# A gate brought ahead of the attention output, and GpSimd's pooling moved in among its load issues

## The chip, the cores and the metric

The kernel runs on one core of a Trainium2 chip. The metric is the device time of one execution in microseconds (us), lower is better.

The core has five engines with separate queues: PE (TensorE, matrix products; its products land in eight PSUM banks), ACT (ScalarE), DVE (VectorE), POOL (GpSimd) and SP. In the traces below ACT, DVE and POOL take their instructions in the order of the program (ACT in slot 1: Ln at 33.53, Relu at 34.20, Exp at 34.68 us, as written). Here POOL issues nearly all loads and also does some additions.

## The reference

For each of 8 batches and 8 heads (576 positions, head size 64), two attentions are added: one on q, k, v averaged over groups of four positions, and one in a band of seven positions. The result, as 4608 rows of 512, goes through a gated layer:

```python
out_d   = softmax_attn(mean4(q), mean4(k), mean4(v))       # 144 positions
x       = repeat4(out_d) + banded_attn(q, k, v)            # |i - j| < 4
gate    = np.maximum(x @ w_gate, 0.0)                      # 512 -> 1536
out     = (gate * (x @ w_val)) @ w_out                     # 1536 -> 512
```

## The kernel before

Heads are taken in pairs (`hp`, 0 to 31), rows in nine chunks of 512. After a short fill, the kernel runs in *slots*: slot `s` holds a quarter of a chunk's gated layer (three blocks of 128 columns), and the attention of pair `hp = s + 4` woven between. The gated layer of one block is two groups of four matmuls into a pair of banks, then a *gate*: Relu on ACT out of the first bank, and a multiply with the second bank on DVE.

```python
    def emit_h(c, jj, pp, parts=...):                 # pp: pair of banks
        h1, h2 = pair(pp)[:, 0, :], pair(pp)[:, 1, :]
        ...                                           # 4 + 4 matmuls
        def gate():
            r1 = ffn.tile([128, TCH], FP16, name="r1", tag="r1")
            nc.scalar.activation(out=r1, in_=h1, func=AF.Relu)
            nc.vector.tensor_tensor(out=gT[c % 2][:, jj, :], in0=r1, in1=h2, op=ALU.mult)
        return gate
```

The last gate of a slot is not emitted there. It is handed to the next slot as `gate`, the *pending gate*. In slots 1 to 5 the next slot passed it into the attention output `emit_s2t`, whose normalisation is a reciprocal by way of logarithms:

```python
    def emit_s2t(hp, between):
        ...                                           # sums to banks 4, 5; products to banks 2, 3
        r, x = rden[r2], xn[r2]
        nc.scalar.activation(out=r, in_=ps[:, 4:6, 0:360], func=AF.Ln)
        between()                                     # the pending gate: Relu on ACT, multiply on DVE
        nc.scalar.activation(out=r, in_=r, func=AF.Exp, scale=-1.0)
        nc.vector.tensor_tensor(out=x, in0=ps[:, 2:4, 0:360], in1=r, op=ALU.mult)   # xn
        emit_xsum(hp)                                                               # xT
```

The scores of the next pair (`emit_s1`, banks 4 to 7) are exponentiated on ACT and masked on DVE in two pieces; the mask multiply has two inputs in SBUF:

```python
            nc.vector.tensor_tensor(out=o, in0=o, in1=_sap(masks_sb, ...), op=ALU.mult)   # ee
```

POOL adds up v in groups of four (pairs 9 and up), in two additions which also have both inputs in SBUF: `v2` (about 1.17 us) and then `v1` (about 0.72 us). Before, both stood at the head of a slot, in front of that slot's load issues:

```python
    def emit_slot(s, gate):
        c, jj, hp = s // 4, 3 * (s % 4), s + LEAD
        if NVP <= hp + 1 < NP:
            emit_vd_pool(hp + 1)                      # v2, v1 on POOL
        emit_in(hp + 4)                               # POOL: issues q, k, then v
        ...
        if s <= 5:
            if s == 5:
                emit_pool(hp)
            elif s < 4:
                emit_vd(hp, 1)
            emit_s2t(hp - 1, gate)
        ...                                           # s 1 to 3: emit_h(jj, pair 0), emit_s1,
                                                      # emit_h(jj + 1, pair 1: banks 2, 3), ...
                                                      # s >= 5: emit_s1 earlier, then emit_s2w(hp)
```

The softmax here doesn't subtract the row's maximum and nothing guards it: scores larger than these inputs give would overflow.

## Time and profile before

| kernel before | |
|---|---|
| time | 354.89 us, median of 3 runs (354.39 to 355.57); 354.70 with a fourth run |
| span of the trace | 352.6 us |
| PE busy | 343.5 us |
| granted PE clock (1.00 is full speed) | 1.00 |

The busy times of the engines, from the first part of the page (engine, us, share of the span, instructions):

```profile
PE 343.5 (97%) x2947; PEld 187.0 (53%) x2947; DVE 248.3 (70%) x397; ACT 214.0 (61%) x370; POOL 189.5 (54%) x233
```

PE is the limit, so only the time in which PE waits can be won. This is its table of waits, cut to three lines (line of PE, whom it waited for, then total us, times, longest us):

```profile
...
PE ps L505 <- DVE xn L426: 0.8, 3, 0.3
...
PE ps L505 <- DVE gT L521: 0.5, 1, 0.5
PE ps L448 <- DVE ee L326: 0.3, 1, 0.3
```

The first is in slots 1 to 3, once each, the last is in slot 5; the middle one is in the tail, after slot 27. The rest of the table lies in the fill. The wait in slot 1, on PE's timeline (start us, duration us, engine, line, operation, tiles, shapes, count, and in brackets the idle time before and who ended it):

```profile
35.93 0.29 PE L314 MATMUL ps<-qkT 64*128 64x96 f16 x6
36.48 1.02 PE L505 MATMUL ps<-xT,wg_sb 128*128 128x512 f16 x4 [0.26 <-DVE xn L426]
```

The bracket says 0.26 us. From start to start it is 36.48 - 35.93 = 0.55 us, while in slots 0 and 4, without a wait, the same step takes 0.22 us; so the loss is 0.33 us (PE's ends are modelled, so starts are the better measure). What PE waits for is `xn`, which reads banks 2 and 3. Here is what ACT did meanwhile:

```profile
33.03 0.37 ACT L294 CAST vd<-ps 72x256 f16<-72x256 f32 x1 [1.52 <-PE ps L287]
33.53 0.77 ACT L423 ACTIVATE rden<-ps 128x720 f32<-128x720 f32 x1
34.20 0.59 ACT L520 ACTIVATE r<-ps 128x512 f16<-128x512 f32 x1
34.68 0.81 ACT L425 ACTIVATE rden<-rden 128x720 f32<-128x720 f32 x1
```

and DVE:

```profile
34.83 0.69 DVE L521 TENSOR_TENSOR gT<-r,ps 128x512 f16<-128x512 f16 x1 [3.24 <-ACT r L520]
35.52 0.91 DVE L426 TENSOR_TENSOR xn<-ps,rden 128x720 f16<-128x720 f32 x1
```

The Relu of the pending gate (L520) stands between Ln (L423) and Exp (L425), and its multiply (L521) stands ahead of xn (L426). Exp ends at 34.68 + 0.81 = 35.49 us and the multiply at 35.52 us: either could be what holds xn up. The trace does not say which, since a wait is put down to the one that came last.

Slot 5 has the other wait. DVE's two masks, POOL's additions, and PE's attention output (one timeline each):

```profile
71.39 2.31 DVE L326 TENSOR_TENSOR ee<-ee,cst_sb 112x576 f16<-112x576 f16 x2
```

```profile
71.03 1.46 POOL L274 TENSOR_TENSOR v<-v 72x512 f32<-72x512 f16 x1
72.56 0.82 POOL L275 TENSOR_TENSOR vd<-v 72x256 f16<-72x256 f32 x1
```

```profile
73.27 0.23 PE L456 MATMUL ps<-ed,vd 72*128 72x72 f16 x2
73.76 0.29 PE L448 MATMUL ps<-ee,vw 112*128 112x96 f16 x3 [0.26 <-DVE ee L326]
```

Two masks take 0.82 us elsewhere. Here they took 2.31 us, and PE had to wait for the second: 0.49 us between these two starts, against 0.07 us in slot 6, a loss of 0.42 us. From about 80 to 279 us PE has no wait at all.

### The profile page before, as it was taken

How to read it: one execution, taken by the hardware profiler on the slowest of the kernel's cores; microseconds unless marked ns; L12 is line 12 of the kernel's file. 1: busy time of each engine (PE TensorE's matmuls, PEld its weight loads, DVE VectorE, ACT ScalarE, POOL GpSimd, SP SyncE). 2: the span in 40 equal slices, each digit the busy share in tenths (PEclk: the TensorE clock that was granted, in tenths of full speed). 3: DMA queues.
4: the chain of work that ended last, by engine and by line, in shares of the span. 5: the costliest groups of instructions: out<-in, count | busy, mean ns of one | idle time of the engine just before them, and what ended most of it. 6: DMA issues, size and time to landing. Idle time of an engine off the chain costs nothing.

```text
span 352.6 us, 7540 instructions
## 1 busy us (share of the span) xinstructions
PE 343.5 (97%) x2947; PEld 187.0 (53%) x2947; DVE 248.3 (70%) x397; ACT 214.0 (61%) x370; POOL 189.5 (54%) x233
## 2 busy tenths in 40 slices
PE   6999999999999999999999999999999999999996
PEld 3665555545545555555555544455555465655575
DVE  5894666687786677788887787776777655354581
ACT  3867776676677766666666667667667533333332
POOL 8986557999999877777778877722100000000000
PEclk9999999999999999999999999999999999999999
DMA  9999999999999999999999999940000000101013
GB/s 153 168 171 187 182 194 153 180 167 194 176 146 166 171 131 131 134 134 118 134 119 138 113 131 140 123 95 30 32 31 32 33 30 30 46 30 46 15 47 119
DMA packets 168770, 40.26 MB, mean 114 GB/s; under 512 B 150080, under 2 KB 165664, under 8 KB 168736
## 3 DMA queue, kind: packets, MB, share of 16 engines
q0 software_dynamic: 132960, 22.93, 86.1%
q1 hardware_dynamic: 32176, 10.55, 17.6%
q10 hardware_dynamic: 3600, 6.32, 5.3%
q8 instruction: 23, 0.38, 0.5%
q14 instruction: 11, 0.09, 0.1%
HBM read 46.45 MB, written 9.44 MB: 159 GB/s over the span
## 4 chain that ended last, share of the span: by engine, by line
PE 89%; DVE 4%; ACT 4%; DMA 1%; issue 1%; POOLq 0%
PE ps L505 50%; PE ps L530 18%; PE ps L592 8%; PE ps L448 3%; PE ps L248 2%; PE ps L314 2%; PE ps L303 2%; PE ps L456 2%; DMA qk<-in_k_dram 1%; DVE xn L426 1%; ACT rden L423 1%; DVE xo L375 1%; ACT rden L425 1%; DVE ee L326 1%; ACT r L520 1%
## 5 line engine op out<-in xcount | busy, mean ns | idle before, releaser
L505 PE MATMUL ps<-xT,wg_sb 128*128 128x512 f16 x432 | 111.5, 379 | 0.9 <-DVE xn L426 0.8
L505 PE MATMUL ps<-xT,wv_sb 128*128 128x512 f16 x432 | 111.2, 379 | 0.5 <-DVE gT L521 0.5
L521 DVE TENSOR_TENSOR gT<-r,ps 128x512 f16<-128x512 f16 x108 | 71.8, 683 | 49.2 <-PE ps L505 32.4
L520 ACT ACTIVATE r<-ps 128x512 f16<-128x512 f32 x108 | 64.0, 593 | 38.2 <-PE ps L505 35.7
L530 PE MATMUL ps<-wo_sb,gT 128*128 128x512 f16 x288 | 70.1, 380 | 0.0
L505 PEld LDWEIGHTS <-wv_sb 128*128 128x128 f16 x432 | 42.1, 98 | 51.4 <-issue 0.8
L472 DVE TENSOR_TENSOR xn<-ps,rden 64x720 f16<-64x720 f32 x46 | 41.6, 905 | 39.2 <-ACT rden L469 38.5
L505 PEld LDWEIGHTS <-wg_sb 128*128 128x128 f16 x432 | 39.7, 97 | 39.5 <-issue 0.7
L323 ACT ACTIVATE ee<-ps 112x576 f16<-112x576 f32 x64 | 38.1, 647 | 26.2 <-PE ps L314 25.4
L466 ACT ACTIVATE rden<-ps 64x720 f32<-64x720 f32 x46 | 35.2, 764 | 12.9 <-PE ps L456 12.3
L530 PEld LDWEIGHTS <-gT 128*128 128x128 f16 x288 | 26.1, 98 | 30.0
L326 DVE TENSOR_TENSOR ee<-ee,cst_sb 112x576 f16<-112x576 f16 x64 | 40.8, 674 | 1.3 <-ACT ee L323 1.1
L275 POOL TENSOR_TENSOR vd<-v 72x256 f16<-72x256 f32 x23 | 17.7, 770 | 44.2 <-PE ps L456 43.5
L194 POOL DMA_DIRECT2D qk<-in_q_dram x46 | 34.1, 744 | 4.2 <-DMA wo_sb<-in_moe_w_out_dram 2.8
L194 POOL DMA_DIRECT2D qk<-in_k_dram x46 | 33.2, 728 | 0.6 <-DMA qk<-in_k_dram 0.4
L215 POOL DMA_DIRECT2D vw<-in_v_dram x30 | 28.4, 946 | 4.9 <-PE ps L396 1.4
L229 DVE TENSOR_REDUCE qkd<-qkT 128x288 f16<-128x1152 f16 x23 | 30.8, 1341 | 0.0
L274 POOL TENSOR_TENSOR v<-v 72x512 f32<-72x512 f16 x23 | 30.5, 1327 | 0.3
L538 ACT COPY y_sb<-ps 128x512 f32<-128x512 f32 x24 | 14.1, 587 | 17.2 <-PE ps L530 17.2
L431 DVE TENSOR_TENSOR xT<-xn 128x576 f16<-128x576 f16 x28 | 22.3, 798 | 0.2
L448 PE MATMUL ps<-ee,vw 112*128 112x96 f16 x276 | 20.4, 205 | 0.3 <-DVE ee L326 0.3
L332 ACT ACTIVATE ed<-ps 72x576 f16<-72x576 f32 x32 | 20.5, 642 | 0.0
(97 smaller groups left out, 374.4 us busy)
## 6 DMA issues: line engine op xcount, KB each, us to landing
out_dram<-y_sb ACTq DMA_DIRECT2D x24, 256.0 KB, 4.0
vw<-in_v_dram POOLq DMA_DIRECT2D x30, 168.0 KB, 6.3
qk<-in_q_dram POOLq DMA_DIRECT2D x46, 72.0 KB, 3.4
qk<-in_k_dram POOLq DMA_DIRECT2D x46, 72.0 KB, 3.6
v<-in_v_dram POOLq DMA_DIRECT2D x23, 144.0 KB, 6.2
out_dram<-y_sb SPq DMA_DIRECT2D x22, 128.0 KB, 1.7
wg_sb<-in_moe_w_gate_dram POOLq DMA_DIRECT2D x4, 384.0 KB, 9.8
wv_sb<-in_moe_w_val_dram POOLq DMA_DIRECT2D x4, 384.0 KB, 10.7
```

What stands on the lines that cost most here:

```text
L194: nc.gpsimd.dma_start(dv[:, :, hh, :], _dap(src, off + hh * S * D, [[D, 96], [NQ * D, NB], [1, D]]),)
L229: nc.vector.tensor_reduce(out=qkd[hp % 2].rearrange("p i t -> p (i t)"), in_=qkT[hp % 4][:, 0 : 2 * S].rearrange("p (t f) -> p t f", f=4), ...
L274: nc.gpsimd.tensor_tensor(out=m, in0=t[:, :, 0:128], in1=t[:, :, 128:256], op=ALU.add)
L323: nc.scalar.activation(out=o, in_=ps[0:WK, p0 + 2 * g : p0 + 2 * g + 2, 0:288], func=AF.Exp, scale=scale)
L326: nc.vector.tensor_tensor(out=o, in0=o, in1=_sap(masks_sb, (0, WK), 288 * g, [[0, 2], [1, 288]]), op=ALU.mult,)
L448: nc.tensor.matmul(out=ps[:, bank, NQ * j : NQ * j + NQ], lhsT=vflat[:, v0 : v0 + 128], rhs=e[:, hh, lo : lo + NQ], start=True, stop=True,)
L466: nc.scalar.activation(out=r[lo : lo + 64], in_=ps[de : de + 64, 4 + 2 * hh : 6 + 2 * hh, 0:360], func=AF.Ln)
L472: nc.vector.tensor_tensor(out=x[lo : lo + 64], in0=ps[lo : lo + 64, 4 + 2 * hh : 6 + 2 * hh, 0:360], in1=r[lo : lo + 64], op=ALU.mult,)
L505: nc.tensor.matmul(out=pair(pp)[:, which, :], lhsT=w[:, kk, bass.ts(jj, 128)], rhs=xT[:, kk, c * TCH : (c + 1) * TCH], start=(kk == 0), st ...
L520: nc.scalar.activation(out=r1, in_=h1, func=AF.Relu)
L521: nc.vector.tensor_tensor(out=gT[c % 2][:, jj, :], in0=r1, in1=h2, op=ALU.mult)
L530: nc.tensor.matmul(out=y_ps, lhsT=gT[c % 2][:, jj, bass.ts(ty, 128)], rhs=wo_sb[:, jj, :], start=(jj == 0), stop=(jj == NJJ - 1),)
```

## The change

The intent is to take ACT's Relu and DVE's multiply out of the way of the normalisation in slots 1 to 4, and to move POOL's additions to another place in its queue. No arithmetic is added or removed.

```diff
-    def emit_load(hp):
+    def emit_load_qk(hp):
         ...                                  # q, k issues
+    def emit_load_v(hp):
         ...                                  # v issues
-    def emit_vd_pool(hp):
+    def emit_v2(hp):                         # first addition, if NVP <= hp < NP
+    def emit_v1(hp):                         # second addition, likewise
@@ emit_in(hp, between=lambda: None)
-        emit_load(hp)
+        emit_load_qk(hp)
+        between()
+        emit_load_v(hp)
@@ emit_slot, VS = 8
-        if NVP <= hp + 1 < NP:
-            emit_vd_pool(hp + 1)
-        emit_in(hp + 4)
+        if s < VS:
+            def pools():
+                emit_v2(hp + 1)
+                emit_v1(hp + 1)
+                if s == VS - 1:
+                    emit_v2(hp + 2)
+            emit_in(hp + 4, pools)
+        else:
+            emit_v1(hp + 1)
+            emit_in(hp + 4, lambda: emit_v2(hp + 2))
@@
-            elif s < 4:
-                emit_vd(hp, 1)
-            emit_s2t(hp - 1, gate)
+            else:
+                gate()
+                if s < 4:
+                    emit_vd(hp, 1)
+            emit_s2t(hp - 1, gate if s == 5 else lambda: None)
```

More of the change, by code (lines that the diff above doesn't have):

```diff
@@ L85 @@
     NVP = 9
+    VS = 8
     NK = NJJ // 2
@@ L197, in emit_load @@
                     )
+    def emit_load_v(hp):
+        r = hp % NL
+        b, off = head_off(hp)
         base = off - 3 * D
@@ L270, in emit_qkT_pe @@
                 copy(out=big[:, i], in_=t[:, :, 0:96])
-    def emit_vd_pool(hp):
-        t, m, o = v4[hp % NV4], v2[hp % 2], vd[hp % 3]
-        nc.gpsimd.tensor_tensor(out=m, in0=t[:, :, 0:128], in1=t[:, :, 128:256], op=ALU.add)
+    def emit_v2(hp):
+        if NVP <= hp < NP:
+            t, m = v4[hp % NV4], v2[hp % 2]
+            nc.gpsimd.tensor_tensor(out=m, in0=t[:, :, 0:128], in1=t[:, :, 128:256], op=ALU.add)
+    def emit_v1(hp):
+        if not NVP <= hp < NP:
+            return
+        m, o = v2[hp % 2], vd[hp % 3]
         nc.gpsimd.tensor_tensor(
@@ L652, with emit_in @@
     after_load = {3: 0, 5: 1, 6: 2, 7: 3}
-    def emit_in(hp):
+    def emit_in(hp, between=lambda: None):
         if hp >= NP:
+            between()
             return
@@ L658, in emit_in @@
             nc.gpsimd.memset(vw[hp][:, :, 64:128], 1.0)
-        emit_load(hp)
+        emit_load_qk(hp)
+        between()
+        emit_load_v(hp)
         if hp in after_load:
```

## The prediction

> **What bounds it now.** TensorE. On the page it is busy 343.5 of 352.6 us, at a granted clock of 1.00. From 80 to 279 us the timeline shows it without a gap, 9.17 us a slot; no gain there. PE's waits add up to some 5.6 us, mostly in the fill or at the tail. The change can reach two groups:
>
> 1. Slots 1, 2 and 3: 0.26 us each before the gate projection into banks 2 and 3 (36.48, 44.77, 53.06 us), released by DVE's xn (L426), which reads those banks. From the last score matmul to that projection it is 0.55 us, against 0.22 us in slots 0 and 4: 3 x 0.33 = 1.0 us lost.
> 2. Slot 5: the attention output waits for the masked ee (L326): 0.49 us between its first two banks at 73.3 us, against 0.07 us in slot 6; 0.42 us lost. The two mask multiplies took 2.31 us there, against 0.82 us with GpSimd idle and about 1.77 us while it issued DMAs; here GpSimd was pooling v (71.0 to 73.4 us).
>
> **What the change does.** No arithmetic is added or removed.
>
> *Gate first.* ScalarE, slot 1: vd cast, Ln (33.53), pending Relu (34.20), Exp (34.68 to 35.49); DVE's xn starts at 35.52. The Relu holds up Exp by its pitch, 0.48 us. Its input is ready before the slot, and ScalarE idled 1.5 us before the vd cast: it moves into idle time. Exp ends near 35.0, xn near 35.95. PE is ready at 36.15: the wait goes, with 0.2 us to spare.
>
> *Pooling amid the loads.* GpSimd's queue is full from 57 us. Adding its durations (q,k issues 2.9, pooling 1.9 to 2.3, v issues 1.7 us), slot 4's pooling falls near 67.4 to 69.4 us and the next near 74, on either side of slot 5's masks (from about 70.4 us). The masks meet only DMA issues: 1.77 us. Slot 5's wait should go, or nearly. The Trainium skill's GPSIMD Engine Reference (1. Specifications) says that GpSimd shares its SBUF interfaces with VectorE and contends with instructions with two SBUF inputs. The trace agrees: L326 and L431 (two SBUF inputs) stretch; L521 and L426 (one in PSUM) stay at 0.69 and 0.91 us.
>
> **What may be given back.** In slot 7 three pooling steps run in one piece, by my count at 87 to 90.5 us, where xT (L431) and the masks fall: perhaps 3.7 us, against 3.3 us from xT's start to PE's need. I put 0.15 us on a new wait of 0 to 0.5 us. From slot 8 on I expect none.
>
> **Sum.** -1.0 (slots 1 to 3), -0.35 (slot 5), +0.15 (slot 7): -1.2 us, all on PE. 354.89 - 1.2 = 353.7 us; range 352.9 to 354.7 (before's runs spread 1.2 us). Faster by over 2% needs 7 us, more than all PE waits: 1%. Within 2%: 98%. Slower by over 2%: 1%.
>
> **What would show each step.** PE's waits no longer list ps L505 <- DVE xn L426; slots 1 to 3 shrink from 8.29 to about 7.96 us. ACT's Exp (L425) follows Ln directly. ps L448 <- DVE ee is gone in slot 5, the masks at about 1.8 us. A new L448 wait near 91 us would be the give-back.
>
> **What would make it wrong.** The Relu delaying Ln; GpSimd's issues falling elsewhere than counted, so that pooling meets other masks; s2w waiting for a later v pooling.

## The result, and the profile after

| | before | after |
|---|---|---|
| time, median of 4 runs | 354.70 us (354.39 to 355.57) | 353.22 us (353.02 to 353.39) |
| span of the trace | 352.6 us | 351.3 us |
| PE busy | 343.5 us | 344.0 us |
| DVE busy | 248.3 us | 238.2 us |

The ratio is 0.9954 (95% interval 0.9935 to 0.9973). A ratio is the mean time of one kernel's runs over that of the other's of the same rounds, so not quite the ratio of the medians quoted. The gain of 1.5 us is small but clear of noise. The prediction was 353.7 us, range 352.9 to 354.7.

PE's table of waits after, in full. What was L505 is now L516, L448 is L459, L426 is L437, L326 is L337; neither the wait on xn nor the one on ee is there any more:

```profile
PE ps L682 <- DVE zero_sb L152: 1.3, 1, 1.3
PE ps L495 <- DVE xo L386: 0.6, 3, 0.2
PE ps L314 <- DVE qkT L275: 0.5, 1, 0.5
PE ps L253 <- ACT ed L343: 0.5, 1, 0.5
PE ps L516 <- DVE gT L532: 0.5, 1, 0.5
PE ps L253 <- DMA qk<-in_k_dram: 0.5, 1, 0.5
```

Slot 1 (PE, ACT and DVE timelines). The whole slot starts 0.21 us later than in the trace of before, from the fill, so compare distances:

```profile
36.13 0.29 PE L325 MATMUL ps<-qkT 64*128 64x96 f16 x6
36.36 1.04 PE L516 MATMUL ps<-xT,wg_sb 128*128 128x512 f16 x4
```

```profile
32.03 0.60 ACT L531 ACTIVATE r<-ps 128x512 f16<-128x512 f32 x1 [0.33 <-PE ps L516]
33.23 0.37 ACT L305 CAST vd<-ps 72x256 f16<-72x256 f32 x1 [0.60 <-PE ps L298]
33.74 0.77 ACT L434 ACTIVATE rden<-ps 128x720 f32<-128x720 f32 x1
34.54 0.80 ACT L436 ACTIVATE rden<-rden 128x720 f32<-128x720 f32 x1
```

```profile
35.38 0.91 DVE L437 TENSOR_TENSOR xn<-ps,rden 128x720 f16<-128x720 f32 x1 [1.73 <-ACT rden L436]
```

The Relu (L531) runs at 32.03 us, in what was idle time; Exp follows Ln; and PE's step is 36.36 - 36.13 = 0.23 us. xn ends at 35.38 + 0.91 = 36.29 us, so only 0.07 us are to spare.

Slot 5 (DVE, POOL, PE): the additions of the slot before come at 68.65 us and are over at 70.62 us, the masks follow at 71.16 us and take 0.81 us for two. The second addition stretched xT instead (L442, 1.24 us in place of 0.76). The masks behind it came later for that, but were over at 71.97 us, 0.64 us before PE took the second bank.

```profile
69.99 1.24 DVE L442 TENSOR_TENSOR xT<-xn 128x576 f16<-128x576 f16 x1
71.16 0.81 DVE L337 TENSOR_TENSOR ee<-ee,cst_sb 112x576 f16<-112x576 f16 x2
```

```profile
68.65 1.17 POOL L280 TENSOR_TENSOR v<-v 72x512 f32<-72x512 f16 x1
69.90 0.72 POOL L286 TENSOR_TENSOR vd<-v 72x256 f16<-72x256 f32 x1
```

```profile
72.54 0.23 PE L467 MATMUL ps<-ed,vd 72*128 72x72 f16 x2
72.61 0.29 PE L459 MATMUL ps<-ee,vw 112*128 112x96 f16 x3
```

Times of single runs of one kernel scatter by 0.3 to 2.9 us, so the sums below are read from traces, in a form that leaves the fill out: the distance between the starts of the attention outputs on PE's timeline, slot to slot.

| us between attention outputs | 1 to 2 | 2 to 3 | 3 to 4 | 4 to 5 | 5's s2t to its s2w | s2w of 5 to s2w of 6 | sum |
|---|---|---|---|---|---|---|---|
| before | 8.29 | 8.29 | 7.96 | 9.72 | 5.96 | 9.58 | 49.80 |
| after | 7.98 | 7.98 | 7.65 | 9.72 | 5.96 | 9.16 | 48.44 |

So slots 1 to 3 give 3 x 0.31 = 0.93 us and slot 5 gives 0.42 us: together 1.36 us (sums are taken before rounding), against 1.48 us between the medians. A check over all that follows the fill: from the start of slot 1's attention output to the start of the last matmul it is, to 0.01 us, 316.00 us in both traces of before, and 314.66 us in both traces of after, both of gate_only, and those of slot5_head and old_from_8 (below). What else differs between these traces lies in the fill: slot 1 starts at 32.8 to 33.3 us.

### The profile page after: what moved, and what is told of

Same layout as the page of the kernel before. It is cut to its first block, busy times and chain, and to the rows that moved or that the text cites. A ratio compares the mean times of both kernels' runs of the same rounds, so it can differ in the third digit from the quotient of the medians.

```text
span 351.3 us, 7538 instructions
## 1 busy us (share of the span) xinstructions
PE 344.0 (98%) x2947; PEld 187.1 (53%) x2947; DVE 238.2 (68%) x397; ACT 214.7 (61%) x370; POOL 186.2 (53%) x233
## 4 chain that ended last, share of the span: by engine, by line
PE 93%; DVE 3%; ACT 1%; DMA 1%; issue 1%; POOLq 0%
PE ps L516 52%; PE ps L541 18%; PE ps L603 8%; PE ps L459 3%; PE ps L325 2%; PE ps L314 2%; PE ps L253 2%; PE ps L467 2%; DMA qk<-in_k_dram 1%; DVE xo L386 1%; PE ps L398 1%; PE ps L298 0%; ACT rden L477 0%; PE ps L495 0%; DVE gT L532 0%
## 5 line engine op out<-in xcount | busy, mean ns | idle before, releaser
L516 PE MATMUL ps<-xT,wv_sb 128*128 128x512 f16 x432 | 111.2, 379 | 0.5 <-DVE gT L532 0.5
L516 PE MATMUL ps<-xT,wg_sb 128*128 128x512 f16 x432 | 111.5, 379 | 0.1
L531 ACT ACTIVATE r<-ps 128x512 f16<-128x512 f32 x108 | 64.0, 593 | 38.5 <-PE ps L516 34.5
L516 PEld LDWEIGHTS <-wv_sb 128*128 128x128 f16 x432 | 42.2, 98 | 51.3 <-issue 0.8
L516 PEld LDWEIGHTS <-wg_sb 128*128 128x128 f16 x432 | 39.6, 97 | 38.7 <-DVE xT L509 0.6
L337 DVE TENSOR_TENSOR ee<-ee,cst_sb 112x576 f16<-112x576 f16 x64 | 29.9, 504 | 1.7 <-ACT ee L334 1.5
L280 POOL TENSOR_TENSOR v<-v 72x512 f32<-72x512 f16 x23 | 27.6, 1201 | 0.2
L442 DVE TENSOR_TENSOR xT<-xn 128x576 f16<-128x576 f16 x28 | 21.7, 777 | 0.2
L459 PEld LDWEIGHTS <-vw 112*128 112x128 f16 x276 | 17.4, 97 | 5.4
```

The lines of the kernel that those rows point to most:

```text
L337: nc.vector.tensor_tensor(out=o, in0=o, in1=_sap(masks_sb, (0, WK), 288 * g, [[0, 2], [1, 288]]), op=ALU.mult,)
L516: nc.tensor.matmul(out=pair(pp)[:, which, :], lhsT=w[:, kk, bass.ts(jj, 128)], rhs=xT[:, kk, c * TCH : (c + 1) * TCH], start=(kk == 0), st ...
```

## The experiments

Twelve kernels ran. "Sum" is the last column of the table above. The runs of before that stand beside them have a median of 354.74 us (11 runs) for the first four, 354.75 us (11 runs) for the second four, and 354.42 us (7 runs) for the last four.

| run | time, us | runs | ratio to before | slots 1, 2, 3 (us) | sum (us) |
|---|---|---|---|---|---|
| gate_only | 353.75 (353.03 to 354.48) | 6 | 0.9968 | 7.98, 7.98, 7.65 | 48.45 |
| pool_only | 354.04 (353.89 to 354.67) | 5 | 0.9980 | 8.29, 8.29, 7.96 | 49.38 |
| gate_last | 357.25 (356.82 to 358.13) | 6 | 1.0066 | 8.84, 8.84, 8.50 | 52.92 |
| slot5_gate | 353.88 (352.82 to 354.54) | 6 | 0.9968 | 7.98, 7.98, 7.65 | 48.33 |
| after_again | 353.24 (352.93 to 353.86) | 6 | 0.9958 | 7.98, 7.98, 7.65 | 48.45 |
| both_more | 352.89 (352.16 to 354.12) | 6 | 0.9949 | 7.98, 7.98, 7.65 | 48.32 |
| memset_pool (wrong results) | 354.17 (354.00 to 354.36) | 4 | 0.9981 | 8.29, 8.30, 7.96 | 49.39 |
| slot5_head | 353.60 (353.28 to 356.21) | 4 | 0.9981 | 7.98, 7.98, 7.65 | 48.46 |
| act_dummy | 354.23 (354.17 to 354.47) | 4 | 0.9993 | 8.32, 8.32, 7.99 | 49.48 |
| old_from_8 | 353.38 (353.10 to 354.55) | 4 | 0.9973 | 7.98, 7.98, 7.65 | 48.45 |
| gate_only_again | 352.94 | 1 | | 7.98, 7.98, 7.65 | 48.45 |
| before_again | 354.74 | 1 | | 8.29, 8.29, 7.96 | 49.80 |

The 95% intervals of memset_pool (0.9961 to 1.0001), slot5_head (0.9950 to 1.0013) and act_dummy (0.9973 to 1.0013) take in 1, so what these three show is in their traces and not in their times.

### The same two kernels once more: after_again, before_again

No edit. They show how far one trace can be trusted.

> The changed kernel once more, on the chip and in the rounds of the three runs below, to see how far one trace can be trusted. Theory: slots 1 to 3 are again 7.98, 7.98 and 7.65 us, since nothing in them depends on a transfer's time; slot 5 again has no wait on ee; about 1.2 us below before. Rival (slot 5's relief hangs on where GpSimd's issues happen to fall, since they wait for earlier transfers): the pooling of slot 4 is displaced by over 0.5 us from 68.65 us, and slot 5's wait can come back.

> A second trace of the kernel before. Theory: slots 1 to 3 again 8.29, 8.29 and 7.96 us with three waits on xn of 0.26 us, since no transfer takes part. Slot 5's wait on ee comes with the pooling at 70.5 to 72 us; if GpSimd is held up by a transfer this time, the pooling and the wait move or vanish.

The slot times repeat to 0.01 us, waits and all. POOL's places do not repeat so well: in the changed kernel the additions ahead of slot 5's masks began at 68.08 us in after_again against 68.65 us, because POOL's issues also wait for earlier transfers. In after_again xT was not stretched, and slot 5 had no wait; in before_again the additions began at 71.20 us (71.03 us in the first trace), the masks again took 2.31 us and the wait was there. The gain is real and repeats: 353.24 us against 354.75 us.

### The gate alone: gate_only

```diff
 # before.py, nothing of the pooling changed
-            elif s < 4:
-                emit_vd(hp, 1)
-            emit_s2t(hp - 1, gate)
+            else:
+                gate()
+                if s < 4:
+                    emit_vd(hp, 1)
+            emit_s2t(hp - 1, gate if s == 5 else lambda: None)
```

> The kernel before with the pending gate ahead of the attention output in slots 1 to 4, and nothing else. Theory (the gate removes the wait on xn in slots 1 to 3): the list of PE waits no longer has the projection waiting for DVE xn; slots 1 to 3 are 0.31 us shorter each, together 0.9 to 1.0 us. For slot 5 there are two views. If GpSimd's pooling still meets the masks that PE needs, 0.2 to 0.4 us of its wait on ee stays and the time is about 1.0 us below before. If PE's being 1 us earlier is enough to move the masks off the pooling, or leaves time for one slow mask, the wait goes here too and the time is about 1.3 us below before. I lean to the second: by my count the first mask starts near 70.4 us, so that the pair ends near 72.2 us and PE needs it at 72.3 us.

Slots 1 to 3 have all of the changed kernel's gain (0.93 us). Slot 5's wait is gone too, which the gate does not touch. Its trace shows DVE's masks, and POOL's queue:

```profile
70.62 0.82 DVE L326 TENSOR_TENSOR ee<-ee,cst_sb 112x576 f16<-112x576 f16 x2
```

```profile
71.76 0.74 POOL L217 DMA_DIRECT2D v<-in_v_dram  x1 [1.63 <-DMA qk<-in_k_dram]
72.52 1.17 POOL L274 TENSOR_TENSOR v<-v 72x512 f32<-72x512 f16 x1
```

The masks stand at the same distance from the start of slot 5's attention output as before (71.39 - 67.18 = 70.62 - 66.41 = 4.21 us), and PE wants them at the same distance as well. So being earlier gives PE's chain no slack in itself: where no mask is stretched, the second one ends 1.12 us before PE takes the second bank, in gate_only, pool_only and after_again alike. What moved is the pooling against it: from 71.03 - 67.18 = 3.85 us to 72.52 - 66.41 = 6.11 us. Of this shift, 0.77 us are PE being earlier, and 1.49 us are POOL being later, held up 1.63 us by a transfer.

### The gate alone, a second trace: gate_only_again

> A second trace of the gate alone. In the first, slot 5 had no wait, but there GpSimd stood 1.6 us waiting for an earlier transfer, so that its pooling began at 72.5 us, behind the masks (70.6 to 71.4 us). Theory A (being 1 us earlier frees slot 5 by itself): no wait on ee again, wherever the pooling falls. Theory B (it was GpSimd's chance delay): if the pooling now begins between 70.4 and 71.4 us, a mask of 1.4 us meets PE and slot 5 waits 0.1 to 0.4 us; with a delay as before, no wait, and the question stays open.

POOL was held up again (0.46 and 0.96 us, by transfers of k), the additions again came at 72.45 us, behind the masks (70.36 to 71.18 us), and slot 5 had no wait. The gate alone thus got both parts of the gain in both traces, but the expected view that being early is enough has not been shown: in neither trace did slot 5's additions meet its masks. The spare of 1.12 us speaks against it: in before the two masks took 1.49 us longer (2.31 against 0.82), more than the spare. By that estimate the gate alone would have kept the wait had POOL not been late; one stretched mask would have fitted. Why POOL is held up there in both traces, and in neither trace of before, is open; it is not the gate's doing alone, since pool_only's POOL, with the gate in its old place, was held up 1.07 us at the same issue.

### The pooling alone: pool_only

```diff
 # after.py, with the gate back in its old place
-            else:
-                gate()
-                if s < 4:
-                    emit_vd(hp, 1)
-            emit_s2t(hp - 1, gate if s == 5 else lambda: None)
+            elif s < 4:
+                emit_vd(hp, 1)
+            emit_s2t(hp - 1, gate)
```

> The changed kernel with the gate back between Ln and Exp: the new places of the pooling, alone. Theory: slots 1 to 3 keep the 0.26 us wait on xn each; in slot 5 the pooling (68.7 to 70.6 us in the changed kernel) is over before the masks start at about 71.4 us, the two masks take 0.8 to 0.9 us and the wait on ee (0.26 us, 0.42 us by start times) is gone: about 0.4 us below before. Rival (the pooling has nothing to do with slot 5's wait, which comes from slots 1 to 3 being late): the wait stays, and the time is that of before.

As expected by the theory: three waits on xn stay, slot 5's goes (the masks took 0.82 us for two), and the sum falls by 0.42 us. The rival is out: slot 5's wait does not come from slots 1 to 3 being late. The two halves of the change do not add up, though: 0.42 us alone, nothing on top of gate_only as its two traces have it.

### What stretches the masks: memset_pool

```diff
 # before.py, pooled v is zero: wrong results on purpose (relative error 0.13)
-        nc.gpsimd.tensor_tensor(out=m, in0=t[:, :, 0:128], in1=t[:, :, 128:256], op=ALU.add)
-        nc.gpsimd.tensor_tensor(out=<vd>, in0=<m>, in1=<m>, op=ALU.add)
+        nc.gpsimd.memset(m, 0.0)
+        nc.gpsimd.memset(m, 0.0)
+        nc.gpsimd.memset(<vd>, 0.0)
+        nc.gpsimd.memset(<vd>, 0.0)
```

> The kernel before, with GpSimd's pooling additions replaced by memsets of the same buffers, two each so that GpSimd stays busy at the same places. Wrong results on purpose (the pooled v is zero). GpSimd then still writes there but reads nothing. Theory (the masks are stretched because GpSimd's additions read the memory through an interface that the masks' second input needs): the masks take 0.45 us each in slot 5 and in the later slots, DVE's busy time falls by about 10 us, slot 5's wait on ee is gone, about 0.4 us below before; slots 1 to 3 keep their wait on xn. Rival 1 (any GpSimd work, or its load issues, stretch the masks): masks of 1.4 us and the wait remain. Rival 2 (ee is late because xn is late): the masks are short, the wait remains.

POOL now writes where it added, and reads nothing. DVE's masks in slot 5, and one of POOL's memsets beneath them:

```profile
71.55 0.82 DVE L323 TENSOR_TENSOR ee<-ee,cst_sb 112x576 f16<-112x576 f16 x2
```

```profile
71.12 0.52 POOL L275 MEMSET v<- 72x512 f32 x1
```

No mask of the 64 took over 0.46 us (before had 16 of over 0.9 us, up to 1.42 us), although memsets lay over 24 of them and load issues over 27. Slot 5's wait is gone, the waits on xn are not, and the sum falls by 0.41 us. Rival 1 is out, as load issues and writes do not stretch a mask; rival 2 is out, as xn was as late as before. This is what the Trainium skill's SBUF — State Buffer says in its section Who interferes with whom: a VectorE instruction with two SBUF inputs contends with a GpSimd instruction that reads SBUF, and not with one that only writes it. The trace agrees with it. It also corrects how the prediction read the masks: the pair of 1.77 us was not two masks slowed by load issues, but one of 1.40 us and one of 0.45 us. Of the thirteen such pairs in before, eleven have an addition shown over the long mask; in the other two (62.88 and 89.48 us) the next addition is shown only 0.25 and 0.06 us after that mask's end (see the last section).

### The pooling of slot 5 back at its head: slot5_head

```diff
 # after.py
-            emit_in(hp + 4, pools)
+            if s == 5:
+                pools()
+                emit_in(hp + 4)
+            else:
+                emit_in(hp + 4, pools)
```

> The changed kernel with the pooling of slot 5 alone put back at the head of the slot, ahead of its q and k issues. GpSimd would then begin it at about 72.3 us by its shown span, 0.3 us after the masks of slot 5 (71.2 to 72.0 us) are over. Theory A (only a shown overlap stretches a mask): masks 0.8 to 0.9 us together, no wait on ee, the time of the changed kernel. Theory B (an addition queued behind load issues already holds up the masks, as one trace of before suggests: a mask at 62.88 us took 1.40 us and was over 0.25 us before the addition's shown start): one mask of 1.4 us, and a wait on ee of 0.1 to 0.4 us.

This run missed its aim. The additions that were moved began at 73.06 us, the masks were over at 72.07 us, and PE had no wait, as theory A has it. But the addition of slot 4, not moved, ran to 71.39 us and stretched one of the masks (1.35 us for the two) all the same, so theory B was not put to a clean test. Slot 7 of this trace speaks for B: xT at 87.72 us took 1.50 us (0.75 alone) and was over 0.13 us before the next addition's shown start. One of its four runs took 356.21 us; that run has no trace. What it does show: a pair of masks of 1.35 us fits into slot 5's slack, one of 2.31 us does not. Slot 5 of slot5_gate and of both_more has the same pair of 1.35 us, also without a wait.

### The order from slot 8 on: old_from_8

```diff
 # after.py
-                if s == VS - 1:
-                    emit_v2(hp + 2)
             emit_in(hp + 4, pools)
         else:
+            emit_v2(hp + 1)
             emit_v1(hp + 1)
-            emit_in(hp + 4, lambda: emit_v2(hp + 2))
+            emit_in(hp + 4)
```

> The changed kernel with the old order of pooling and loads from slot 8 on, where PE is dense in all traces. Theory: masks of 1.4 us come back in those slots (ten or more), DVE's busy time rises by 7 to 10 us, PE has no wait there and the time is that of the changed kernel within 0.2 us. Rival (the order matters in the later slots too): waits of PE on ee in slots 8 and up, 0.3 us or more in total.

DVE's busy time is back at that of before, 15 masks are stretched, and PE's table of waits is the changed kernel's, line for line but for the first load's time:

```profile
PE 343.5 (98%) x2947; PEld 187.0 (53%) x2947; DVE 248.1 (71%) x397; ACT 214.6 (61%) x370; POOL 189.4 (54%) x233
```

So the 10 us that DVE saves in the later slots are worth nothing on PE.

### Which of the two held xn up: act_dummy

```diff
 # after.py
+    scratch = keep.tile([128, 512], FP16, name="scratch")
+    def emit_dummy():
+        nc.scalar.activation(out=scratch, in_=zero_sb[:, 0:512], func=AF.Relu)
-            emit_s2t(hp - 1, gate if s == 5 else lambda: None)
+            emit_s2t(hp - 1, gate if s == 5 else emit_dummy)
```

> The changed kernel (gate first) with a ScalarE instruction of the Relu's kind and size, which nobody waits for, put between Ln and Exp in slots 1 to 4, where the Relu was. DVE is free of the gate's multiply by then. Theory (what held xn up was ScalarE's instruction between Ln and Exp, and there are only about 0.07 us to spare): Exp starts 0.4 us later in the slot than in the changed kernel, less about 0.1 us that Exp waits for Ln anyway; the projection's wait on xn is back in slots 1 to 3 with 0.2 to 0.3 us each, 0.6 to 0.9 us above the changed kernel. Rival (DVE's multiply just ahead of xn was what held it up; the two ended within 0.03 us of each other in before): no wait, the time of the changed kernel.

The gate is done early, DVE is free, and an idle Relu stands where the gate's Relu was. ACT in slot 1, and PE's wait:

```profile
33.57 0.77 ACT L435 ACTIVATE rden<-ps 128x720 f32<-128x720 f32 x1
34.23 0.62 ACT L702 ACTIVATE scratch<-zero_sb 128x512 f16<-128x512 f16 x1
34.75 0.79 ACT L437 ACTIVATE rden<-rden 128x720 f32<-128x720 f32 x1
```

```profile
PE ps L517 <- DVE xn L438: 0.9, 3, 0.3
```

DVE stood idle before xn, and what ended its wait was Exp:

```profile
35.58 0.91 DVE L438 TENSOR_TENSOR xn<-ps,rden 128x720 f16<-128x720 f32 x1 [2.10 <-ACT rden L437]
```

All three waits are back, slots 1 to 3 are 8.32, 8.32 and 7.99 us, 0.03 us longer even than before. By the sums that is 1.04 us above after, a little more than the 0.6 to 0.9 us expected. So ACT's instruction between Ln and Exp is enough to cause the whole wait, without DVE's multiply. (That the multiply alone would not have done it is not shown: it cannot run before its Relu.) Slot 5's wait stays away here with PE as late as before: the pooling came at 67.53 us, and the masks took 0.82 us.

### Late in place of early: gate_last

```diff
 # after.py: the gate after Exp and xn, in slots 1 to 4
-        between()
+        if not late:
+            between()
         nc.scalar.activation(out=r, in_=r, func=AF.Exp, scale=-1.0)
         nc.vector.tensor_tensor(out=x, in0=ps[:, 2:4, 0:360], in1=r, op=ALU.mult)
+        if late:
+            between()
         emit_xsum(hp)
 ...                                                  # emit_slot: late in slots 1 to 4, no gate ahead
```

> The changed kernel, but in slots 1 to 4 the pending gate comes after Exp and after xn, and not ahead of everything. xn is then as early as in the changed kernel. Theory (the gate must be early and not merely out from between Ln and Exp, since banks 6 and 7 that it reads are wanted by the score matmuls that follow): PE no longer waits on xn, but the score matmuls of slots 1 to 3 wait for the gate's DVE multiply (gT), by 0.5 to 0.9 us each; 1.5 to 2.7 us above the changed kernel, slower than before by 0.2 to 1.2 us. Rival (any order with Exp right behind Ln is as good): within 0.2 us of the changed kernel.

PE's waits, cut to what is new:

```profile
PE ps L314 <- DVE gT L535: 1.9, 3, 0.6
...
PE ps L462 <- DVE ee L337: 1.1, 2, 0.5
...
PE ps L544 <- DVE gT L535: 0.4, 1, 0.4
```

The wait on xn is gone, but the score matmuls now wait for the gate to leave banks 6 and 7, and slots 1 to 3 are 8.84, 8.84 and 8.50 us, 0.86 us longer than after. The size I gave for the sum was too small: the kernel is 4.0 us behind after (357.25 against 353.22 us; 4.5 us by the sums, its traced run being the slowest of six), since slot 4's output product also waits for the gate (0.4 us) and in slot 5 the attention output waits for both masked pieces (1.1 us): a mask there at 75.05 us took 1.40 us, beside an addition at 74.48 us. Even with the new order of pooling, then, a PE that is over 3 us later (slot 5 starts at 69.88 us against 66.45 us) brings masks and additions together again.

### Two more waits: slot5_gate, both_more

slot5_gate puts the gate first in slot 5 as well; both_more also gives the first tail slot's projections the other pair of banks.

```diff
 # slot5_gate, from after.py
             if s == 5:
                 emit_pool(hp)
-            else:
-                gate()
-                if s < 4:
-                    emit_vd(hp, 1)
-            emit_s2t(hp - 1, gate if s == 5 else lambda: None)
+            gate()
+            if s < 4:
+                emit_vd(hp, 1)
+            emit_s2t(hp - 1, lambda: None)
 # both_more, on top: first tail slot, pairs of banks swapped
-                emit_h_mm(c, jj, 0, 0, range(3))
-                emit_h_mm(c, jj, 0, 1, range(3))
+                emit_h_mm(c, jj, 1, 0, range(3))
+                emit_h_mm(c, jj, 1, 1, range(3))
                 w.p2()
                 ...                                    # then pairs 1, 0, 1 in place of 0, 1, 0
```

> The changed kernel with the gate of slot 5 also ahead of the attention output, behind that slot's pooling of q and k. In the changed kernel slot 5's second pair of score matmuls is stretched: 0.63 us from the first score matmul to the next projection, 0.50 us in slot 6, because bank 7 is being read by the gate's multiply. Theory: that 0.13 us goes, the time is 0.1 us below the changed kernel, and xn of slot 5 starts 0.3 to 0.7 us earlier in the slot. Rival (the stretch is not the gate's): the 0.63 us stays.

> The changed kernel with two further edits: slot 5's gate ahead of its attention output too (-0.13 us, seen in the run before), and in the first tail slot the projections take the other pair of banks first, so that their first one no longer waits 0.52 us for the pending gate's multiply to leave bank 1. Theory: the wait of the projection on DVE gT, 0.5 us at about 280 us, goes and nothing takes its place: 0.6 to 0.7 us below the changed kernel, about 1.9 us below before. Rival (the wait moves to the output product p2, which needs the same gT): the list of PE waits shows the output matmuls waiting for gT by up to 0.5 us, and 0.1 us is gained.

In slot 5 the step from the first score matmul to PE's next group falls from 0.63 us to 0.50 us, and xn starts 0.35 us earlier in the slot, as expected. That slot5_gate is 0.1 us faster is not shown by its times: its median, 353.88 us, is above after's 353.22 us, from other rounds. In the tail, PE after and PE in both_more:

```profile
278.90 0.81 PE L516 MATMUL ps<-xT,wg_sb 128*128 128x512 f16 x3
280.23 0.81 PE L516 MATMUL ps<-xT,wv_sb 128*128 128x512 f16 x3 [0.52 <-DVE gT L532]
```

```profile
278.90 0.81 PE L516 MATMUL ps<-xT,wg_sb 128*128 128x512 f16 x3
279.63 0.81 PE L516 MATMUL ps<-xT,wv_sb 128*128 128x512 f16 x3
```

The wait is gone and does not come back elsewhere: the step is 0.73 us in place of 1.33 us. From slot 1 to the last matmul both_more takes 313.94 us, after takes 314.66 us, before 316.00 us. Its median, 352.89 us, is the lowest of all kernels; against after_again, measured on the same chip in the same rounds (353.24 us), it is 0.35 us lower where 0.6 to 0.7 us were expected, and the runs overlap, so the 0.7 us rest on the traces.

## Why the prediction was right

- **What bounds the kernel: right.** The whole gain lies in PE's waits, and it is small because those waits are.
- **Gate first, -1.0 us: right, 0.93 us measured.** The wait went in all three slots, the Relu fell into idle time, and act_dummy shows that ACT's instruction between Ln and Exp was enough to cause it. The spare was put at 0.2 us and is 0.07 us: Exp was taken to start one pitch (the distance between two starts: 0.67 us, as for the Relu) after Ln, but it reads what Ln writes, and starts 0.80 us after it (34.54 - 33.74), when Ln has ended. Had that cost 0.1 us more, a part of the wait would have stayed.
- **Slot 5, -0.35 us: right, 0.42 us measured.** The reason, additions on POOL against masks on DVE, holds (pool_only, memset_pool). The step that "the masks meet only DMA issues: 1.77 us" was wrong: load issues do not slow masks, which took 0.81 us. Nor was it seen that in the traces of the gate alone, with POOL late, this wait would be gone too. The places were off as well: slot 4's additions came at 68.65 to 70.62 us, 1.2 us later than counted, and ended just where the masks would have begun (at 70.61 us in after_again); they met xT. That no mask was met was in part luck, but the slack would have borne one (slot5_head).
- **Slot 7's give-back, +0.15 us: not there.** The three additions and the masks did meet, as counted; here are DVE's masks after and the first of POOL's three additions, which run on to 91.65 us:

```profile
88.33 2.31 DVE L337 TENSOR_TENSOR ee<-ee,cst_sb 112x576 f16<-112x576 f16 x2
```

```profile
88.22 1.20 POOL L280 TENSOR_TENSOR v<-v 72x512 f32<-72x512 f16 x1
```

  But POOL came 1.2 us later than counted, xT was spared (0.75 us), and the masks ended at 90.64 us, 0.30 us before PE took the second bank at 90.94 us: from xT's start 2.97 us, where 3.7 us were counted, against 3.3 us of room. The margin is thin. In slot5_head's trace xT was stretched there too, with one mask, and 3.19 us left 0.08 us to spare.
- **The sum** was -1.2 us, the traces show -1.36 us, the medians -1.48 us. The prediction's difference is the give-back that did not come.

Open: the runs of one kernel scatter by up to 2.9 us. gate_only's six runs lie at 353.0 to 353.2 and at 354.3 to 354.5 us; none of the upper group was traced, so where they lose their time is not known.

## What to carry to other kernels

When an engine with slack has an instruction for somebody else in the middle of a chain that a full engine waits for, move it to where that engine idles, ahead of the chain and not behind it: earlier saved 0.31 us a slot, later cost 0.55 us a slot. Before counting on a change that makes a side engine 10 us faster, look whether the full engine ever waits for it; here two of the 16 stretched masks mattered, both in slot 5. And test the halves of a change one by one: their gains need not add up, and one may, as here by a late POOL, seem to do the work of both.

## What the Trainium skill lacked or had wrong

- SBUF — State Buffer (SBUF: two separate sides) says that of a VectorE instruction with two SBUF inputs and a GpSimd instruction that reads SBUF, whichever starts first keeps the shared pair of ports for its whole duration, and the other blocks fully. The runs agree in kind and give sizes that the page lacks: a mask of 0.45 us took 1.40 us against the first addition (1.17 us alone) and 0.98 us against the second (0.72 us alone), and in before each of the 14 masks stretched under a shown addition was over 0.32 to 0.33 us after that addition's shown end.
- No page says how far ahead of its shown start an addition on GpSimd can already hold up VectorE. In before a mask that started at 62.88 us took 1.40 us and was over at 64.27 us, 0.25 us ahead of the shown start of the next addition (64.52 us), with only load issues shown beside it, and the mask at 89.48 us likewise; memset_pool shows that load issues do not do this. Perfetto Trace Analysis (GPSIMD Engine Instruction) puts the shown start where the first DSP issues its read, and says that each of the eight DSPs keeps its own queue, so others may have begun before it; no run here settles it.
- No page gives ScalarE's pitch for a dependent instruction: Exp, reading what Ln wrote, started 0.80 us after Ln, while an independent Relu started 0.67 us after it. In after, each of the 27 Exps that directly follow their Ln started 0.03 us after its shown end; the Relu of before started 0.10 us ahead of it.
